# A two-layer Fourier-mixing and attention kernel: four roundings spread over four steps, statistics split, DFT weights loaded two steps later, and three output projections without maxima

## The chip, the cores and the metric

The kernel runs on one core of one Trainium2 chip. The metric is device microseconds (us) of one execution; for the kernel before there are three runs, and one more execution was profiled. TensorE is called PE here (PEld are its weight loads), VectorE DVE, ScalarE ACT, GpSimd POOL; SP is SyncE, which issues most DMAs. Each engine takes its instructions in the order in which they were written for it, so an instruction that waits holds up all that is behind it on its engine.

## The reference

All data is float32. `x` has 2048 rows (the sequence) of 512 features. Two layers, each a Fourier mixing and an attention, follow each other:

```python
def A(x):                                   # Fourier mixing, real part
    a = x @ dft_hid_re.T ; b = x @ dft_hid_im.T
    return dft_seq_re @ a - dft_seq_im @ b  # 2048 x 2048 matrices
def B(x):                                   # 32 heads of 16; one shared k and v
    q = (x @ wq) split in 32 heads ; k = x @ wk ; v = x @ wv
    p = softmax(q k^T / 4)                  # 2048 x 2048 per head
    return (p v, heads joined) @ wo
x = x + A(layernorm(x)); x = x + B(layernorm(x))
x = x + A(layernorm(x)); x = x + B(layernorm(x))
```

## The kernel before

**Products in three parts.** A float32 operand is split in a rounded part and a rest (`h` and `l`), and a product is three matmuls: h·h, h·l, l·h. Making such a pair takes a rounding (ACT, "CAST" in the trace) and a subtraction (DVE or POOL).

**The Fourier stage** (`phase_a`, once per layer) does the sequence DFT first. It has 128 steps `n`: four row blocks `tb` of the result; in each, 16 sequence blocks of the real matrix (`c` = 0), then 16 of the imaginary one (`c` = 1). In step `n` the matrix tile for step n+6 is loaded (`c_load`, into `craw`, three buffers), that for step n+2 is split (`c_split`, into `ch` on ACT and `cl` on POOL, or on DVE in the first 20 steps of layer 0; four buffers), and PE does 12 matmuls of 128 rows (tb = 0), or 24 of 64 rows (from tb = 1 on, two steps at a time, in two phases `ph`; from n = 112 on with 256 columns). They accumulate in four PSUM banks `z`, in two pairs (tile `x` in the trace). After the first phase ACT copies two columns (`junk`), and the second phase waits for that.

**The turn from c = 0 to c = 1.** After the 16th block, `evac` copies the four banks to row buffers (ACT, "ACTIVATE row<-x"), which frees the banks for c = 1, rounds all four to `zh` (ACT, "CAST slot<-row"), and subtracts for `zl` (two on POOL, two on DVE, "TENSOR_TENSOR slot<-row,slot"). All of it is written before the next steps' roundings of `ch`. The turn is taken four times in a layer.

**After c = 1** `y_rows` multiplies by the feature DFT matrix (`dh`, `dl`; loaded by `d_load`, split by `d_split` in tb = 0, in eight pieces through two row buffers, so that load j waits until piece j-2 is split), adds x (four additions on DVE, two after each PSUM pair), and takes the layernorm statistics of four tiles (`ln_stats`: bn_stats and bn_aggr), from which `ln_rstd` makes the scale. In the next row block's steps (`prep_tasks`) come transposes, k and v (`kv`, `v_tr`) and the queries (`q_mm`), which are stored to DRAM (`qd`). In layer 0, `load_wkv` at n = 20 loads the k and v weights and rounds them at once.

**Early maxima.** Softmax needs the maximum of each row of scores. A maximum is one matmul into a bank of tag `y` (three banks) or `z` (one) and one DVE reduce of 128x512. PE has room for them between the Fourier matmuls: `feed` issues a pair wherever the estimate `Pace` finds the banks free. The table `EARLY` says for which query tile and key block, in which slot, when the tile is loaded (`qT_load` at step n0), and from which place to which place (40 per row block) pairs may be fed. Which tag is taken depends on the place within the row block.

**The attention stage** (`phase_b`) has 16 query tiles of 32 steps. A step is four score matmuls, exp on ACT, four products with v (L900), and on average three of the maxima that later tiles need (`more_max`, in the order of `units`). `owed` keeps the count at 3 per step plus `o.extra`. At step 12 of tile i the projection of tile i-1 is done (`o_proj`, 12 matmuls), and after its second and fourth block two extra maxima each. A tile's maxima become mask rows (`max_neg` five steps before the tile, `max_rows`, the DMA `slot<-mt`). The query tile 13 is loaded at step 2 of tile 11, into the slot that tile 10 has just left.

Of the kernel before, what the change touches and what calls it, by code (L numbers as in the profile page):

```python
# [22 lines left out]
NT = S // P  # L23
# [9 lines left out]


EARLY = [
# [12 lines left out]
def fnet_mqa_kernel(ctx: ExitStack, tc: tile.TileContext, x_in, ct, dt_, wq, wkv, wo, out):  # L48
# [6 lines left out]
    def f(ap):  # L55
        return ap.bitcast(F32)
# [18 lines left out]
    def mm(out_, w, x, **k):  # L75
        shape_to(x.shape[0])
        Pace.pe += free(x) / 512 * (0.117 if x.shape[0] <= 64 else 0.233)
        nc.tensor.matmul(out_, w, x, **k)  # L78
# [27 lines left out]
    vec, act, pool = Timed(nc.vector, "dve"), Timed(nc.scalar, "act"), Timed(nc.gpsimd, "pool")  # L106
# [4 lines left out]
    def half(k, dtype=F32):  # L111
        return sb.tile([P, D], dtype, name=f"row{k}")
# [8 lines left out]
    def pair():  # L121
        return ps.tile([P, 2, 512], F32, name="x", bufs=2)

    def split_ps(ps_, hi, lo, neg=False):
        act.activation(hi, ps_, AF.Copy, scale=-1.0 if neg else 1.0)
        if neg:
            vec.scalar_tensor_tensor(lo, ps_, -1.0, f(hi), op0=ALU.mult, op1=ALU.subtract)
        else:
            vec.tensor_sub(lo, ps_, f(hi))

    def split_sb(raw, hi, lo, eng=None):
        act.copy(hi, raw)
        (eng or vec).tensor_sub(lo, raw, f(hi))
# [54 lines left out]
    def ln_stats(x, t):  # L188
        st = sb.tile([P, 6], F32, name="bst", bufs=2)
        vec.bn_stats(st, x)  # L190
        vec.bn_aggr(mv[:, t, :], st)
# [58 lines left out]
    def make_layer(L, src, mid, dst, last):  # L250
# [8 lines left out]
        def where(n):  # L259
            return n // 32, (n // 16) % 2, n % 16  # L260
# [27 lines left out]
        def d_load(j):  # L288
            st["d", j] = half(4 + j % 2)
            nc.sync.dma_start(st["d", j], dt_[j // NK][:, j % NK, :])  # L290

        def d_split(j):
            c, k = divmod(j, NK)
            split_sb(st["d", j], dh[c][:, k, :], dl[c][:, k, :])
# [95 lines left out]
        def partial(i):  # L390
            if i not in o.mxp:
                o.mxp[i] = sb.tile([P, NPAIR, 2, 4 if i else 5], F32, name=f"mxp{i % 4}")
                for e, (i_, kb) in enumerate(KEPT):
                    if i == i_:
                        np_ = taken[i, kb]
                        if np_:
                            pool.tensor_copy(o.mxp[i][:, :np_, :, kb], st["mxe"][:, e, :np_])
            return o.mxp[i]

        def max_pair(i, pr, c0, n, to, tags="yy"):  # L400
            pm = [bank(tag)[:, :n] for tag in tags]
            for g in range(2):
                gs = slice(64 * g, 64 * g + KR)
                mm(pm[g], o.qT[i][gs, pr, :], kz[gs, c0:c0 + n], start=True, stop=True)
            for g in range(2):
                vec.reduce_max(to[:, g:g + 1], pm[g], axis=AX.X)
                read(tags, g, Pace.dve)
# [10 lines left out]
        def feed():  # L418
            e = next((e for e in ahead if EARLY[e][4] <= Pace.at < EARLY[e][5]), None)
            if e is None:  # L420
                return
            n = Pace.at % 40
            tags = "zy" if n > 6 and Pace.z < Pace.y[1] else "yy"
            if max(Pace.z if tags == "zy" else Pace.y[1], Pace.y[0]) > Pace.pe + 0.3:
                return
            pr = ahead[e].pop(0)
            i, kb = EARLY[e][:2]
            if "mxe" not in st:
                st["mxe"] = sb.tile([P, len(KEPT), NPAIR, 2], F32, name="mxe")
            to = partial(i)[:, pr, :, kb] if i < 4 else st["mxe"][:, KEPT.index((i, kb)), pr]  # L430
            max_pair(i, pr, kb * 512, 512, to, tags)
            if not ahead[e]:
                del ahead[e]
# [48 lines left out]
        def y_rows(tb, zh, zl, x1, between):  # L482
            yp = [pair(), pair()]
            at = 0
            for ph in range(2):
                for cc in range(2):
                    for a in range(2):
                        for kk, k in enumerate((0, 2, 1, 3)):
                            for t in range(3):
                                for r in range(2):  # L490
                                    j = (r + ph) % 2
                                    rs_ = slice(64 * r, 64 * r + 64)
                                    ts_ = slice((2 * a + j) * P, (2 * a + j + 1) * P)
                                    w = (zl if t == 2 else zh)[cc][rs_, k, ts_]
                                    mm(yp[a][:, j, :], w, (dl if t == 1 else dh)[cc][rs_, k, :],
                                                     start=ph == cc == kk == t == 0, stop=cc == 1 and kk == 3 and t == 2,
                                                     skip_group_check=True)
                                between(at)
                            at += 1
                        if cc == 1 and ph == 0:  # L500
                            act.copy(junk, yp[a][:, :, 0])
                        elif cc == 1:
                            for j in range(2):
                                vec.tensor_add(x1[2 * a + j], yp[a][:, j, :], x1[2 * a + j])
                                pool.dma_start(mid[4 * tb + 2 * a + j], x1[2 * a + j])
            for tt in range(4):
                ln_stats(x1[tt], 4 * tb + tt)

        def y_tile(tb, tt, zh, zl, x1, between={}):
# [127 lines left out]
        def phase_a(extra):  # L637
# [5 lines left out]
            def add(n, fn):  # L643
                tasks.setdefault(n, []).append(fn)
# [9 lines left out]
                    add(14 + 2 * t, lambda t=t: qd_zero(t))  # L654
            add(1, d_alloc)
            for j in range(8):
                add(15 + j, lambda j=j: ((d_split(j - 2) if j > 1 else None), d_load(j)))
            add(23, lambda: d_split(6))
            add(24, lambda: d_split(7))
            inner = {}  # L660

            def by_rows(n):
# [5 lines left out]
            zh, zl, x1, vt = {}, {}, {}, {}  # L668
# [25 lines left out]
            def y_early():  # L694
                more = {k: [feed, feed] for k in (1, 4, 7)}
                y_tile(3, 0, zh, zl, x1[0], more)
                y_tile(3, 1, zh, zl, x1[1], more)
# [30 lines left out]
            held = []  # L728

            def evac(c, ds, cols):  # L730
                if cols != slice(0, 512):
                    for d in ds:
                        split_ps(z[d][:, cols], zh[c][:, d, cols], zl[c][:, d, cols], neg=c == 1)
                    return
                for k, d in enumerate(ds):
                    r = half((0 if tb == c == 0 else 4) + 2 * k + int(ds[0] > 0))
                    act.activation(r, z[d], AF.Copy, scale=-1.0 if c else 1.0)
                    held.append((d, r, vec if k and not c else pool))
                if c or len(held) == 4:
                    for d, r, eng in held:  # L740
                        act.copy(zh[c][:, d, :], r)
                        eng.tensor_sub(zl[c][:, d, :], r, f(zh[c][:, d, :]))
                    held.clear()

            def within(n, k, t):
# [34 lines left out]
            for n in range(128):  # L780
                tb, c, s = where(n)
# [12 lines left out]
                if n >= 112:  # L794
                    ch, cl = hls.pop(n)
                    h, sp = divmod(n - 112, 8)
# [59 lines left out]
        def more_max():  # L856
            if o.done < len(units) and units[o.done][0] in o.loaded | {0}:
                max_half(*units[o.done])
                o.done += 1
# [89 lines left out]
        def o_mm(k):  # L949
            if k == 0:  # L950
                bt["po"] = bank("y")
            ks = slice(k * P, (k + 1) * P)
            mm3(bt["po"], bt["oh"][:, ks], bt["ol"][:, ks], woh[:, k, :], wol[:, k, :], k == 0, k == NK - 1)

        def o_proj(i):
            for k in range(NK):
                o_mm(k)
                if k == NK - 1:
                    o_add(i)
                if k % 2 and i < NT - 1:  # L960
                    for _ in range(2):
                        more_max()
                        o.extra += 1

        def o_add(i):
            nc.vector.tensor_add(bt["x"], bt["po"], bt["x"])
            (nc.sync if last else nc.gpsimd).dma_start(dst[i], bt["x"])
# [128 lines left out]

        woh = wol = osp = None
        o.phase_a, o.phase_b = phase_a, phase_b
        return o

# [45 lines left out]
```

## Time and profile before

| what | value |
|---|---|
| runs | median 3648.55 us (3647.73 to 3650.05, 3 runs) |
| the profiled execution | 3649.77 us, its span 3648.0 us |
| granted TensorE clock, mean | 0.993 |
| busy share of the span | PE 98%, PEld 53%, DVE 77%, ACT 65%, POOL 21% |
| layer 0, Fourier stage | 0 to 664 us of the span |
| layer 0, attention stage | 664 to 1831 us |
| layer 1, Fourier stage | 1831 to 2473 us |
| layer 1, attention stage | 2473 to 3648 us |

The span runs from the first to the last instruction; what lies around it is 1.77 us in the profiled execution. A matmul counts as busy for longer than it holds up the next one: two matmuls of 64 rows run side by side, and a pair of them follows the pair before after 0.233 us, though each is shown with 0.39 us. So time that PE loses is read from the idle times in brackets, from the starts of matmuls, and from the granted clock.

### The profile page before, as it was taken

The numbers are of one execution on the slowest core, as the hardware profiler recorded it, in microseconds if no ns is written. First come the engines' busy times: TensorE is split into PE (matmuls) and PEld (weight loads), VectorE is DVE, ScalarE is ACT, GpSimd is POOL, SyncE is SP. The second block draws the span as 40 slices with busy tenths as digits, with TensorE's granted clock in tenths as the row PEclk, the third lists the DMA queues.
The fourth block names the chain that finished last, engine by engine and source line by source line (L and its number), as shares of the span: only waits on it lengthen the run. The fifth ranks groups of instructions, "written<-read, shape, count | busy, mean of one in ns | idle before, by whom it ended". The sixth has DMA issues, their size and how long they took to land.

```text
span 3648.0 us, 63760 instructions
## 1 busy us (share of the span) xinstructions
PE 3571.4 (98%) x25090; PEld 1924.1 (53%) x25090; DVE 2801.7 (77%) x4819; ACT 2389.4 (65%) x3058; POOL 782.6 (21%) x976
## 2 busy tenths in 40 slices
PE   8999999999999999999999999999999999999999
PEld 6777878434333333334377878773343334333433
DVE  6176988888888888888311869878888888888881
ACT  3322232788888888888943232328888888888888
POOL 5544342111121112111254343420000000000000
PEclk9999999999999999999999999999999999999999
DMA  5544242311111100110143343422111111001100
GB/s 171 133 149 122 88 128 73 85 48 34 36 34 39 43 25 22 31 51 22 42 128 104 122 127 103 130 65 75 47 36 34 34 48 34 25 21 50 33 24 26
DMA packets 204445, 240.85 MB, mean 66 GB/s; under 512 B 36848, under 2 KB 160752, under 8 KB 197232
## 3 DMA queue, kind: packets, MB, share of 16 engines
q1 hardware_dynamic: 199216, 219.98, 20.3%
q0 software_dynamic: 4864, 16.78, 1.6%
q8 instruction: 196, 3.21, 0.4%
q14 instruction: 105, 0.86, 0.1%
q10 hardware_dynamic: 64, 0.02, 0.0%
HBM read 172.48 MB, written 63.17 MB: 65 GB/s over the span
## 4 chain that ended last, share of the span: by engine, by line
PE 84%; DVE 7%; ACT 2%; issue 1%; DMA 1%; SPq 0%; POOL 0%; ACTq 0%; DVEq 0%; POOLq 0%
PE z L900 26%; PE y L78 19%; PE x L886 19%; PE x L78 17%; DVE mxp L102 4%; PE z L78 1%; DVE mxe L102 1%; ACT slot L889 1%; ACT slot L881 0%; DVE slot L102 0%; PE z L83 0%; DMA slot<-qd 0%; PE y L879 0%; DVE bst L102 0%; DVE row L102 0%
## 5 line engine op out<-in xcount | busy, mean ns | idle before, releaser
L102 DVE TENSOR_REDUCE mxp<-y 128x1 f32<-128x512 f32 (+1 forms) x3464 | 2160.9, 678 | 271.8 <-PE y L78 216.5
L889 ACT ACTIVATE slot<-x 128x1024 f32<-128x1024 f32 x1984 | 1938.2, 1028 | 327.3 <-PE x L886 249.8
L900 PE MATMUL z<-slot,v 128*32 128x512 f32 x8192 | 1097.8, 606 | 2.4 <-ACT row L903 2.4
L78 PE MATMUL y<-kz,slot 64*128 64x512 f32 (+1 forms) x3040 | 984.3, 426 | 10.1 <-DMA slot<-qd 4.3
L886 PE MATMUL x<-slot,kz 64*128 64x512 f32 x2944 | 886.8, 448 | 2.8 <-DMA slot<-mt 2.7
L886 PEld LDWEIGHTS x<-slot,kz 64*128 64x128 f32 x2944 | 367.1, 185 | 734.3 <-ACT slot L889 594.6
L78 PE MATMUL x<-ch,xnh 64*128 64x512 f32 (+2 forms) x2048 | 543.5, 374 | 22.6 <-ACT xnh L102 9.4
L78 PEld LDWEIGHTS y<-kz,slot 64*128 64x128 f32 x3040 | 490.1, 186 | 126.6 <-DVE mxp L102 32.2
L78 PE MATMUL x<-ch,xnl 64*128 64x512 f32 (+2 forms) x2048 | 540.6, 367 | 1.7 <-POOL xnl L102 1.2
L78 PE MATMUL x<-cl,xnh 64*128 64x512 f32 (+2 forms) x2048 | 536.7, 366 | 1.7 <-POOL cl L102 1.6
L940 POOL TENSOR_TENSOR row<-row,row 128x256 f32<-128x256 f32 x63 | 46.2, 733 | 1581.6 <-DMA row<-rd 987.4
L102 POOL TENSOR_TENSOR cl<-craw,ch 128x512 fp32r<-128x512 f32 x244 | 317.6, 1318 | 288.2 <-ACT ch L102 259.4
L78 PEld LDWEIGHTS x<-ch,xnh 64*128 64x128 f32 (+1 forms) x2048 | 304.7, 187 | 76.0 <-issue 16.2
L78 PEld LDWEIGHTS x<-ch,xnl 64*128 64x128 f32 (+1 forms) x2048 | 310.7, 187 | 37.1 <-POOL xnl L102 5.0
L78 PEld LDWEIGHTS x<-cl,xnh 64*128 64x128 f32 (+1 forms) x2048 | 306.7, 187 | 33.6 <-POOL cl L102 2.9
L900 PEld LDWEIGHTS z<-slot,v 128*32 128x32 f32 x8192 | 164.4, 108 | 276.1 <-issue 248.1
L102 ACT CAST ch<-craw 128x512 fp32r<-128x512 f32 x264 | 158.6, 620 | 173.1 <-PE x L78 152.9
L102 ACT COPY junk<-x 128x2 f32<-128x2 f32 x236 | 37.6, 159 | 354.7 <-PE x L78 336.3
L102 DVE TENSOR_REDUCE mxe<-y 128x1 f32<-128x512 f32 x408 | 256.1, 676 | 6.4 <-PE y L78 6.1
L78 PE MATMUL y<-slot,slot 128*128 128x512 f32 x816 | 218.2, 407 | 9.4 <-DVE mxp L102 7.1
L78 PEld LDWEIGHTS y<-slot,slot 128*128 128x128 f32 x816 | 144.3, 188 | 65.6 <-issue 29.5
L102 DVE TENSOR_REDUCE mxp<-z 128x1 f32<-128x512 f32 x128 | 86.8, 678 | 91.6 <-PE y L78 87.6
(126 smaller groups left out, 2676.9 us busy)
## 6 DMA issues: line engine op xcount, KB each, us to landing
craw<-ct_in SPq DMA_DIRECT2D x112, 512.0 KB
slot<-qd SPq DMA_DIRECT2D x42, 1024.0 KB
qd<-row SPq DMA_DIRECT2D x144, 128.0 KB
od<-row SPq DMA_DIRECT2D x252, 64.0 KB
row<-x_in SPq DMA_DIRECT2D x32, 256.0 KB
mid<-row POOLq DMA_DIRECT2D x32, 256.0 KB, 2.5
craw<-ct_in SPq DMA_DIRECT2D x32, 256.0 KB
row<-mid SPq DMA_DIRECT2D x32, 256.0 KB
```

Of the source, the lines that this page charges most:

```text
L78: nc.tensor.matmul(out_, w, x, **k)
L102: return fn(out_, in_, *a, **k)
L886: nc.tensor.matmul(st["e"][:, g, :], kz[64 * g:64 * g + KR, c * P:(c + 1) * P], o.qT[i][64 * g:64 * g + KR, cp:cp + 4, :], start=True, sto ...
L889: nc.scalar.activation(ptiles[i, s_][:, 2 * w:2 * w + 2, :], st.pop("e"), AF.Exp, scale=DH ** -0.5)
L900: nc.tensor.matmul(a[32 * j:32 * j + 32, :], v1[:, c, :], pt[:, j, :], start=c == 0, stop=c == NT - 1)
L940: nc.gpsimd.tensor_mul(bt["ot"][:, cs], bt["ot"][:, cs], bt["den"][:, cs])
```

## The change

Five things change:

- The table's first four entries (tiles 2, 3, 0 and 1, key block 0) may be fed from 55.5, 60, 63 and 66 on instead of 54.5, 58, 60 and 63, and the bank `z` is used for maxima only from place 7 of a row block on, not from 6.
- In `y_rows` the statistics of the first tile are taken between the first two additions and the last two.
- `d_load` and `d_split` come two steps later (loads at n = 17 to 24).
- At the turn from c = 0, the four roundings with their subtractions are handed out to the steps n+1 to n+4, one to each.
- The projections of tiles 0, 1 and 2 have no extra maxima, and `o.extra` isn't counted up there.

```diff
-    (2, 0, 2, 43, 54.5, 70), (3, 0, 3, 46, 58, 70), (0, 0, 8, 48, 60, 89), (1, 0, 9, 52, 63, 91),
+    (2, 0, 2, 43, 55.5, 70), (3, 0, 3, 46, 60, 70), (0, 0, 8, 48, 63, 89), (1, 0, 9, 52, 66, 91),
...
-            tags = "zy" if n > 6 and Pace.z < Pace.y[1] else "yy"
+            tags = "zy" if n > 7 and Pace.z < Pace.y[1] else "yy"
...
                                 pool.dma_start(mid[4 * tb + 2 * a + j], x1[2 * a + j])
-            for tt in range(4):
+                            if a == 0:
+                                ln_stats(x1[0], 4 * tb)
+            for tt in range(1, 4):
                 ln_stats(x1[tt], 4 * tb + tt)
...
-                add(15 + j, lambda j=j: ((d_split(j - 2) if j > 1 else None), d_load(j)))
-            add(23, lambda: d_split(6))
-            add(24, lambda: d_split(7))
+                add(17 + j, lambda j=j: ((d_split(j - 2) if j > 1 else None), d_load(j)))
+            add(25, lambda: d_split(6))
+            add(26, lambda: d_split(7))
...
             def evac(c, ds, cols):
+                zh_, zl_ = zh.get(c), zl.get(c)
...
+                def low(d, r, eng):
+                    act.copy(zh_[:, d, :], r)
+                    eng.tensor_sub(zl_[:, d, :], r, f(zh_[:, d, :]))
+
+                if c:
+                    for h in held:
+                        low(*h)
+                elif len(held) == 4:
+                    for k, h in enumerate(held):
+                        add(n + 1 + k, lambda h=h: low(*h))
                 if c or len(held) == 4:
-                    for d, r, eng in held:
-                        act.copy(zh[c][:, d, :], r)
-                        eng.tensor_sub(zl[c][:, d, :], r, f(zh[c][:, d, :]))
                     held.clear()
...
-                if k % 2 and i < NT - 1:
+                if k % 2 and 3 <= i < NT - 1:
                     for _ in range(2):
                         more_max()
                         o.extra += 1
```

The numbers of instructions stay nearly the same: one pair of early maxima fewer in each layer, and two maxima more in its attention stage.

Where the instructions stand shows at three places. The first is ACT at the first turn (tb = 0, layer 0), from the four evacuations on. `slot_622` is `zh`, `slot_278` and `slot_280` are the DFT weights, `ch` is the next steps' matrix. Before:

```order
L102 ACTIVATE row_642<-x 128x512
L102 CAST slot_622<-row_630 128x512
L102 CAST slot_622<-row_632 128x512
L102 CAST slot_622<-row_640 128x512
L102 CAST slot_622<-row_642 128x512
L102 CAST ch<-craw 128x512 x2
L102 CAST slot_278<-row_652 128x512
L102 CAST ch<-craw 128x512
L102 CAST slot_278<-row_676 128x512
L102 CAST ch<-craw 128x512
L102 CAST slot_278<-row_696 128x512
L102 CAST wkvh<-row_760 128x512
```

After:

```order
L102 ACTIVATE row_642<-x 128x512
L102 CAST ch<-craw 128x512
L102 CAST slot_622<-row_630 128x512
L102 CAST ch<-craw 128x512
L102 CAST slot_622<-row_632 128x512
L102 CAST ch<-craw 128x512
L102 CAST slot_622<-row_640 128x512
L102 CAST ch<-craw 128x512
L102 CAST slot_278<-row_684 128x512
L102 CAST slot_622<-row_642 128x512
L102 CAST ch<-craw 128x512
L102 CAST wkvh<-row_752 128x512
```

A rounding of the matrix stands between any two of the turn's roundings, and ahead of the k and v weights (`wkvh`) stands one piece of the DFT weights instead of three.

The second is ACT at the turn of tb = 1, layer 0; `slot_1860` is `zh`. Before:

```order
L102 ACTIVATE row_1952<-x 128x512
L102 CAST slot_1860<-row_1928 128x512
L102 CAST slot_1860<-row_1930 128x512
L102 CAST slot_1860<-row_1950 128x512
L102 CAST slot_1860<-row_1952 128x512
L102 CAST ch<-craw 128x512 x2
L102 COPY junk<-x 128x2 x2
```

After:

```order
L102 ACTIVATE row_1940<-x 128x512
L102 CAST ch<-craw 128x512 x2
L102 COPY junk<-x 128x2 x2
L102 CAST slot_1860<-row_1902 128x512
L102 CAST slot_1860<-row_1904 128x512
L102 CAST ch<-craw 128x512 x2
L102 COPY junk<-x 128x2 x2
```

The roundings of `ch` and the copy that lets the second phase begin have moved ahead of the four.

The third is PE in step 5 of tile 11 of layer 0's attention stage. The second operand of an L78 row is the query tile whose maxima are taken. Before (`slot_14407` is tile 12, `slot_16856` is tile 13):

```order
L900 MATMUL z<-slot_16862,v_74 32x512 x4
L886 MATMUL x<-slot_13589,kz 128x512
L78 MATMUL y<-kz,slot_14407 128x512
L886 MATMUL x<-slot_13589,kz 128x512
L78 MATMUL y<-kz,slot_16856 128x512 x2
L886 MATMUL x<-slot_13589,kz 128x512 x2
```

After (`slot_14365` is tile 12; L896 and L910 are the L886 and L900 of before):

```order
L910 MATMUL z<-slot_16820,v_74 32x512 x4
L896 MATMUL x<-slot_13547,kz 128x512
L78 MATMUL y<-kz,slot_14365 128x512
L896 MATMUL x<-slot_13547,kz 128x512
L78 MATMUL y<-kz,slot_14365 128x512 x2
L896 MATMUL x<-slot_13547,kz 128x512 x2
```

Tile 12's maxima are still going on; tile 13's first one stands five steps later, in step 10.

## The prediction

> **What bounds the kernel now.** I read the page first: busy shares and the chain of work that ended last.
>
> ```profile
> PE 3571.4 (98%) x25090; PEld 1924.1 (53%) x25090; DVE 2801.7 (77%) x4819; ACT 2389.4 (65%) x3058; POOL 782.6 (21%) x976
> ...
> PE 84%; DVE 7%; ACT 2%; issue 1%; DMA 1%; SPq 0%; POOL 0%; ACTq 0%; DVEq 0%; POOLq 0%
> ```
>
> PE is the bound nearly everywhere, and the change takes only a fraction of a microsecond of matmuls away. So it can gain only time in which PE stands still or runs slowly, and that is short: what matters is which waits these are. The table of PE's waits (first 130 to 664 us, layer 0's Fourier stage; then 1831 to 2473, layer 1's) gives total, count and longest:
>
> ```profile
> PE x L78 <- ACT junk L102: 4.2, 4, 1.4
> PE z L78 <- DMA slot<-qd: 3.4, 1, 3.4
> PE z L83 <- DVE row L102: 2.5, 3, 0.8
> ...
> PE z L83 <- DVE mxp L102: 0.7, 1, 0.7
> ```
>
> ```profile
> PE x L78 <- ACT junk L102: 4.3, 4, 1.4
> PE z L83 <- DVE row L102: 2.6, 3, 0.9
> ```
>
> (The row on `z L83 <- DVE mxp` reads the same in layer 1.) Each of these names a place that the change touches. Two costs stand beside them: an earlier wait at 80 us, and the granted clock, which falls to half for some microseconds behind longer waits. I take the parts in the order of the program.
>
> **(a) DFT weights later, first turn of layer 0.** Timeline of SP, ACT and PE, then busy times with the clock:
>
> ```profile
> 69.94 0.33 SPq L290 DMA_DIRECT2D row<-dt_in  x1
> ...
> 76.66 0.42 SPq L185 DMA_DIRECT2D row<-wkv_in  x1
> 74.43 0.62 ACT L102 CAST slot<-row 128x512 fp32r<-128x512 f32 x1 [8.09 <-DMA row<-dt_in]
> 82.05 0.62 ACT L102 CAST wkvh<-row 128x512 fp32r<-128x512 f32 x1 [6.47 <-DMA row<-wkv_in]
> 83.76 0.80 PE L78 MATMUL x<-ch,xnh 128*128 128x512 f32 x1 [3.81 <-ACT ch L102]
> 84.00:90.00 6.00, 5.36 (x13) 3.84 (x14) 2.12 (x2) 1.90 (x5) 5.08 (x5) 0.53 0.54 167
> ```
>
> ACT waits 8.09 us for the third piece of the DFT matrix, whose load could be issued only at 69.94, when the first piece had been split. SP is held by these loads, and so issues the load of the k and v weights at 76.66 only; ACT, which rounds them at once, stands until 82.05, and the next `ch` is behind it. PE loses 3.81, and then 6 us at a clock of 0.53 lose 6 x 0.47 = 2.8: 6.6 in all. Changed, SP has two loads fewer ahead of the k and v weights, and ACT one piece of DFT weights instead of three. The last thing SP waits for is then the split of the first piece, in step 19. A step is 12 x 0.233 = 2.8 us, and ACT works about one step ahead of PE: PE's step 23 was due at 79.8, so ACT's step 19 falls near 67 and the load is issued near 69. With the latency seen (82.05 - 76.66 = 5.4) it lands near 75, and the `ch` that PE needs at 79.8 is rounded by about 77. Gain 6.6. Ends: 0, if the load still comes late, and 7. The later pieces now wait up to step 26; PE needs them in `y_rows` after step 31, and ACT's cover is the one step by which `ch` runs ahead. Without it each late piece would cost PE what it is late.
>
> **(b) Tile 2's first maxima one step later.** The chain, PE's timeline and the clock:
>
> ```profile
> 193.78 6.07 DMA slot<-qd
> 199.98 0.76 PE L78 MATMUL z<-kz,slot 64*128 64x512 f32 x1 [3.42 <-DMA slot<-qd]
> 200.00:206.00 6.00, 6.00 (x30) 5.11 (x32) 3.88 (x7) 0.16 (x1) 0.00 (x0) 0.52 1.02 427
> ```
>
> The load lands at 199.85 and PE has waited 3.42. The load's place is not moved; the first maximum stands one step, 24 matmuls x 0.117 = 2.8 us, later. 0.6 us of the wait stay, and I take it that the clock doesn't fall for so little: 2.8 + 6 x 0.48 = 5.7. Ends 2.8 (the clock falls all the same) and 6.3. In layer 1 this wait isn't in the table, so nothing there. The other three entries move alike; their tail runs 24 matmuls further into `y_rows`, where DVE is idle.
>
> **(c) The turns.** ACT, DVE and PE at the turn of tb = 1, one subtraction alone elsewhere, the turn at n = 112; then PE's and DVE's busy times, (x) counts instructions, the number behind POOL's is the clock:
>
> ```profile
> 208.96 2.18 ACT L102 CAST slot<-row 128x512 fp32r<-128x512 f32 x4
> 210.20 3.00 DVE L102 TENSOR_TENSOR slot<-row,slot 128x512 fp32r<-128x512 f32 x2 [1.83 <-ACT slot L102]
> 75.09 0.69 DVE L102 TENSOR_TENSOR slot<-row,slot 128x512 fp32r<-128x512 f32 x1 [4.57 <-ACT slot L102]
> 212.29 0.50 PE L78 MATMUL x<-ch,xnh 64*128 64x512 f32 x2 [1.08 <-ACT junk L102]
> 542.97 0.39 PE L78 MATMUL x<-ch,xnh 64*128 64x256 f32 x2 [1.43 <-ACT junk L102]
> ```
>
> ```profile
> 209.00:219.00 10.00, 7.98 (x63) 5.40 (x61) 8.80 (x12) 4.63 (x11) 7.29 (x6) 1.00 0.17 56
> 219.00:229.00 10.00, 10.00 (x89) 8.42 (x88) 10.00 (x18) 1.88 (x6) 3.76 (x3) 1.00 0.50 175
> 372.00:382.00 10.00, 8.08 (x52) 5.79 (x50) 9.09 (x12) 3.82 (x9) 6.63 (x5) 0.83 0.15 52
> 2019.00:2029.00 10.00, 7.99 (x50) 5.57 (x49) 8.79 (x12) 3.62 (x9) 6.65 (x5) 0.83 0.24 85
> ```
>
> Undisturbed, 10 us hold 89 matmuls. The turn at 209 has 63 and loses 26/8.9 = 2.9; the turns at 372 and 2019 lose 37/8.9 = 4.2 and 4.4, of which 10 x 0.17 = 1.7 is a fallen clock. The fourth (layer 1, tb = 2) I take like the first: 14.4 together. Two causes: the `junk` copy is behind four roundings (it comes forward, so that wait goes), and DVE, idle 1.83 for the first rounding, then takes 3.00 for two subtractions while maxima are due. DVE is busy 10.00 of 10 afterwards, so what it loses itself PE does not get back. Spread, DVE's idle time goes; the two subtractions cost between 2 x 0.69 and 3.00, so of the 2.9 between 1.3 and 2.9 come back. I take 2.1, the middle: POOL, whose subtractions coincide with DVE's where it is slow, is busy 7.29 of 10 in the turn's window and 3.76, half of that, in the next, into which the change moves them. 4 x 2.1 + 2 x 1.4 for the clock = 11.2. At n = 112 only the `junk` wait counts: 1.43, twice with layer 1: 2.9. Sum 14.1; ends 8.1 (four times 1.3, no clock) and 17.3. The row buffers are held up to four steps longer; their next users (row block inputs, transposes) come 10 steps later.
>
> [...]
>
> **(d) Statistics split.** DVE's timeline at the end of tb = 0:
>
> ```profile
> 131.92 1.29 DVE L102 TENSOR_TENSOR row<-x,row 128x512 f32<-128x512 f32 x2 [37.48 <-PE x L78]
> 134.54 1.29 DVE L102 TENSOR_TENSOR row<-x,row 128x512 f32<-128x512 f32 x2 [1.33 <-issue]
> 135.74 0.68 DVE L102 BATCH_NORM_STATS2 bst<-row 128x6 f32<-128x512 f32 x1
> 136.56 0.66 DVE L102 BATCH_NORM_STATS2 bst<-row 128x6 f32<-128x512 f32 x1
> ```
>
> One tile's statistics take 136.56 - 135.74 = 0.82 and fit in the 1.33 that DVE waits. All behind them, to the transposes, comes 0.82 earlier; each of the six waits `z L83 <- DVE row` is about 0.83, so 6 x 0.8 = 4.8 go. Ends 3 and 4.9.
>
> **(e) Bank `z` from place 7 on.** The transposes of v need the bank that a maximum has just taken: 0.7 in each layer, 1.4. End 0, if DVE is late with the `y` banks instead.
>
> **(f) to (h) The attention stage.** PE's timeline in tile 11 of both layers, then chain rows: a projection with and one without extra maxima, two steps in a row with three maxima and two without:
>
> ```profile
> 1483.80 0.80 PE L78 MATMUL y<-kz,slot 64*128 64x512 f32 x2 [3.13 <-DMA slot<-qd]
> 3290.95 0.50 PE L78 MATMUL y<-kz,slot 64*128 64x512 f32 x2 [1.15 <-DMA slot<-qd]
> ```
>
> ```profile
> 1276.17 4.06 PE y L78 x16
> 1792.23 3.00 PE y L78 x12
> 1271.72 0.99 PE z L900 x8
> 1273.84 1.00 PE z L900 x8
> 1780.77 1.04 PE z L900 x8
> 1782.66 1.04 PE z L900 x8
> ```
>
> (f) Tile 13's first maximum waits 3.13 and 1.15 for its load. Twelve extra maxima fewer and two units more put it five steps of 1273.84 - 1271.72 = 2.12 later, 10 us: both waits go, and with the first a clock fall, priced at 2.8 like (a): 7.1. (g) Three projections shorter by 4.06 - 3.00 = 1.06, in two layers: 6.4. (h) The 14 maxima come at the end, where a step of 1.89 becomes one of 2.12: 14 x 0.23 / 3 = 1.1, twice: -2.2. Ends for the three: 8 and 12.
>
> **Sum.** 6.6 + 5.7 + 14.1 + 4.8 + 1.4 + 7.1 + 6.4 - 2.2 = 43.9. The profiled execution took 3649.77, 1.77 of it around its span and 1.2 above the median: 3605.9 on its scale, 3604.7 on the median's. I say 3604.5.
>
> **Rivals.** (1) The first turn's wait only moves: load 69 plus a latency as for the third piece, or a later piece holds `ch`. Then (a) is 0: 3611. The 8.09 and 6.47 of ACT speak for it, the two steps won against it. (2) DVE keeps the turns: its 10.00 of 10 speaks for it. (c) falls to 8.1: 3610.5. (3) The change doesn't do what it says in the Fourier stage: the moved maxima meet DVE or their loads a step later, so that (b), (c) and (e), 21.2, are given back: 3626. Against it: the waits have other causes than the amount of maxima. (4) Slower: the maxima lose their lead. The last one of tile 14 stands 4.5 steps ahead of its `max_neg` now, and directly ahead of it then; if mask rows came late at every boundary, PE would wait there, which now costs 2.7 us in all:
>
> ```profile
> L886 PE MATMUL x<-slot,kz 64*128 64x512 f32 x2944 | 886.8, 448 | 2.8 <-DMA slot<-mt 2.7
> ```
>
> One step late, 2.1, at 30 boundaries is 64 us: 3668. It decides from 1.5 us a boundary on (44/30). Against it: DVE takes its work in order and had other tiles' maxima before `max_neg` anyway.
>
> **Chances.** Forecast 0.64, own range 3597 to 3613 (ends of (b) and (c)); rival 1 0.12, rival 2 0.13, rival 3 0.06, slower 0.02, about nothing 0.03. 0.2% (7 us) is about what a measurement can tell from no change. Faster 0.95, same 0.03, slower 0.02. The range: all upper ends give 3600, and the waits not priced here a little less; the lower ends of (a) and (c) together give 3617; 3597 to 3620 leaves out rivals 3 and 4.
>
> **What would show it.** Right: no wait of PE for ACT near 80 us and none over 1 us near 197; no `ACT junk` wait at the turns of n = 48, 80, 112; `z L83 <- DVE row` near 0.1 each; no `slot<-qd` wait in tile 11; projections of tiles 0 to 2 as x12. Wrong: new waits of PE for `DVE mxp` in the turns, `slot<-dt` waits on ACT that reach PE, or `slot<-mt` waits at many boundaries.

## The result, and the profile after

| | before | changed |
|---|---|---|
| median (runs) | 3648.91 us (3647.73 to 3650.05, 4) | 3601.3 us (3600.53 to 3602.6, 4) |
| ratio, 95% interval | | 0.987 (0.9853 to 0.9887) |
| profiled execution / span | 3649.77 / 3648.0 | 3602.02 / 3600.2 |
| mean granted clock | 0.993 | 0.997 |
| layer 0 Fourier, attention | 664.4, 1166.9 | 641.2 (-23.2), 1159.0 (-7.8) |
| layer 1 Fourier, attention | 641.6, 1162.8 | 630.0 (-11.7), 1157.8 (-5.0) |

A stage is counted here from the last exp of the attention stage before it (or the span's start) to its first exp, an attention stage from its first to its last exp. The changed kernel is faster by 47.6 us; the forecast was 3604.5, range 3597 to 3620. The terms of the prediction, laid out by stage, are 22.4, 8.0, 10.1 and 3.3: each stage gained about what it was to gain, the two of layer 1 some 1.7 more.

The page after, then PE's waits in 130 to 629 us (layer 0), then in 1795 to 2436 us (layer 1):

```profile
PE 3551.6 (99%) x25090; PEld 1901.3 (53%) x25090; DVE 2801.6 (78%) x4819; ACT 2390.8 (66%) x3050; POOL 781.9 (22%) x976
...
PE 85%; DVE 7%; ACT 2%; issue 1%; DMA 1%; SPq 0%; POOL 0%; DVEq 0%; ACTq 0%; POOLq 0%
```

```profile
PE z L83 <- DVE row L102: 2.0, 3, 0.8
...
PE x L78 <- ACT junk L102: 0.7, 1, 0.7
...
PE z L78 <- DMA slot<-qd: 0.2, 1, 0.2
```

```profile
PE z L83 <- DVE row L102: 2.1, 3, 0.9
...
PE x L78 <- ACT junk L102: 0.7, 1, 0.7
```

Of the `junk` waits one is left in each layer (step 120, not a turn; 0.66). The wait for `slot<-qd` fell from 3.4 to 0.2, that for `mxp` at `z L83` (0.7) is gone. What did not go is the row on `z L83 <- DVE row`: 2.5 became 2.0, where 0.3 was expected.

Windows of the changed kernel: around the first turn's old wait, behind tile 2's first maxima, and around the four later turns (now 8 to 31 us earlier); the clock is the number behind POOL's count:

```profile
74.00:84.00 10.00, 10.00 (x45) 8.10 (x44) 3.44 (x4) 4.16 (x8) 5.33 (x5) 1.00 0.54 170
200.00:206.00 6.00, 6.00 (x56) 5.13 (x54) 5.97 (x11) 2.60 (x6) 3.99 (x3) 1.00 0.34 111
...
201.00:211.00 10.00, 10.00 (x88) 8.27 (x88) 9.97 (x17) 3.38 (x8) 6.76 (x5) 1.00 0.43 161
360.00:370.00 10.00, 9.53 (x80) 7.76 (x78) 9.97 (x16) 3.29 (x8) 5.76 (x5) 1.00 0.20 63
1994.00:2004.00 10.00, 9.89 (x84) 7.48 (x83) 10.00 (x17) 2.76 (x7) 4.20 (x4) 1.00 0.57 209
2152.00:2162.00 10.00, 9.53 (x80) 7.57 (x78) 10.00 (x15) 2.81 (x8) 5.40 (x4) 1.00 0.17 52
```

The turns hold 88, 80, 84 and 80 matmuls where before held 50 to 63, and no clock falls in them. The two with 80 are those of tb = 2: there PE still waits 0.37 for a maximum (`mxe`) in each layer, where before it waited 0.84. In the chain of work, the projection of tile 0: in a kernel with the old projections (told of below), then in the changed one:

```profile
739.05 4.06 PE y L78 x16
```

```profile
739.10 2.97 PE y L78 x12
```

In tile 11 the table of PE's waits has no row on `slot<-qd` left.

### The profile page after: what moved, and what is told of

Its sections match the earlier page's. It is cut to its first block, busy times and chain, and to the rows that moved or that the text cites. A ratio compares the mean times of both kernels' runs of the same rounds, so it can differ in the third digit from the quotient of the medians.

```text
span 3600.2 us, 63751 instructions
## 1 busy us (share of the span) xinstructions
PE 3551.6 (99%) x25090; PEld 1901.3 (53%) x25090; DVE 2801.6 (78%) x4819; ACT 2390.8 (66%) x3050; POOL 781.9 (22%) x976
## 4 chain that ended last, share of the span: by engine, by line
PE 85%; DVE 7%; ACT 2%; issue 1%; DMA 1%; SPq 0%; POOL 0%; DVEq 0%; ACTq 0%; POOLq 0%
PE z L910 27%; PE y L78 19%; PE x L896 19%; PE x L78 17%; DVE mxp L102 4%; PE z L78 1%; DVE mxe L102 1%; ACT slot L899 1%; PE z L83 1%; ACT slot L891 0%; PE y L889 0%; DVE row L102 0%; DVE bst L102 0%; DVE ms L102 0%; PE y L83 0%
## 5 line engine op out<-in xcount | busy, mean ns | idle before, releaser
L910 PE MATMUL z<-slot,v 128*32 128x512 f32 x8192 | 1096.4, 605 | 1.7 <-ACT row L913 1.7
L78 PE MATMUL y<-kz,slot 64*128 64x512 f32 (+1 forms) x3048 | 980.1, 424 | 4.4 <-DVE kz L102 2.1
L896 PE MATMUL x<-slot,kz 64*128 64x512 f32 x2960 | 891.2, 447 | 0.8 <-DMA slot<-mt 0.8
L896 PEld LDWEIGHTS x<-slot,kz 64*128 64x128 f32 x2960 | 368.1, 185 | 734.3 <-ACT slot L899 599.7
L78 PEld LDWEIGHTS y<-kz,slot 64*128 64x128 f32 x3048 | 487.8, 185 | 121.8 <-DVE mxp L102 26.5
L78 PE MATMUL x<-ch,xnh 64*128 64x512 f32 (+2 forms) x2048 | 531.6, 372 | 11.7 <-ACT xnh L102 9.5
L78 PE MATMUL x<-ch,xnl 64*128 64x512 f32 (+2 forms) x2048 | 527.8, 364 | 1.0 <-POOL xnl L102 0.6
L78 PE MATMUL x<-cl,xnh 64*128 64x512 f32 (+2 forms) x2048 | 524.3, 364 | 0.4 <-POOL cl L102 0.4
L78 PEld LDWEIGHTS x<-ch,xnh 64*128 64x128 f32 (+1 forms) x2048 | 293.1, 185 | 63.4 <-issue 16.2
L78 PEld LDWEIGHTS x<-ch,xnl 64*128 64x128 f32 (+1 forms) x2048 | 298.7, 185 | 38.0 <-POOL xnl L102 4.4
L78 PEld LDWEIGHTS x<-cl,xnh 64*128 64x128 f32 (+1 forms) x2048 | 295.0, 185 | 32.2 <-POOL cl L102 0.7
L910 PEld LDWEIGHTS z<-slot,v 128*32 128x32 f32 x8192 | 163.7, 108 | 274.6 <-issue 247.5
L78 PE MATMUL y<-slot,slot 128*128 128x512 f32 x816 | 216.4, 406 | 8.2 <-DVE mxp L102 6.7
L78 PEld LDWEIGHTS y<-slot,slot 128*128 128x128 f32 x816 | 144.7, 188 | 63.1 <-issue 28.2
L896 PE MATMUL x<-xnl,kz 64*128 64x512 f32 x512 | 154.5, 443 | 0.3 <-DMA xnl<-mt 0.3
```

Source lines behind the costliest of these rows:

```text
L896: nc.tensor.matmul(st["e"][:, g, :], kz[64 * g:64 * g + KR, c * P:(c + 1) * P], o.qT[i][64 * g:64 * g + KR, cp:cp + 4, :], start=True, sto ...
L910: nc.tensor.matmul(a[32 * j:32 * j + 32, :], v1[:, c, :], pt[:, j, :], start=c == 0, stop=c == NT - 1)
```

## The experiments

Each kernel's time is a median, of runs taken beside runs of the kernel before. The changed kernel itself was run again with the second and the third group, to be held against on the same chip.

### The parts alone, in the kernel before

**The turn alone.**

```diff
 (kernel before, with the new evac)
...
+                    for k, h in enumerate(held):
+                        add(n + 1 + k, lambda h=h: low(*h))
```

> The kernel before with one part of the change alone: the four roundings of a turn handed out to the steps n+1 to n+4. Theory (term c): every ACT junk wait at the turns of n = 48, 80 and 112 goes, and with it the DVE mxp or mxe wait behind it (0.84) and the fallen clock; between 14.1 and 17.3 us come back: 3632 to 3635. The wait of PE for ACT near 80 us of layer 0 (3.8, and a halved clock behind it) stays, since the DFT weights are loaded as before. Rival (DVE keeps the turns): 8.1 come back, 3641, and mxp or mxe waits of 0.8 stay at the turns.

Measured 3624.48 us (ratio 0.9934, 0.9922 to 0.9947): 24.9 less, far more than 17.3. Its waits, layer 0:

```profile
PE z L78 <- DMA slot<-qd: 4.7, 1, 4.7
PE z L83 <- DVE row L102: 2.5, 3, 0.8
...
PE x L78 <- POOL cl L102: 0.9, 1, 0.9
...
PE z L83 <- DVE mxp L102: 0.7, 1, 0.7
```

```profile
78.89 0.62 ACT L102 CAST wkvh<-row 128x512 fp32r<-128x512 f32 x1 [7.63 <-DMA row<-wkv_in]
```

The `junk` waits at the turns and the maxima's waits of 0.84 behind them are gone. In layer 1, where nothing else differs, the stage is 6.9 shorter. Taken from the wait of one row block's transposes (`z L83`, behind `y_rows`) to that of the next, its three later row blocks gained 3.3 (1.7 of it a clock fall that is gone), 1.7 and 2.4, or 7.4 in all, where term (c) has 7.05 for a layer. The first row block gained 1.0 (a wait of 0.6 for `cl` is gone), and behind the last of these waits 1.5 is lost, where the clock of this run falls once more, at 2429 us.

The 2.4 are the turn at n = 112, for which the prediction counted only the wait of 1.43. The stretch from the wait ahead of it to the one at step 120, before and then here:

```profile
540.33 0.39 PE L78 MATMUL x<-ch,xnh 64*128 64x256 f32 x2 [0.24 <-ACT row L102]
586.51 0.39 PE L78 MATMUL x<-ch,xnh 64*128 64x256 f32 x2 [0.66 <-ACT junk L102]
```

```profile
528.23 0.39 PE L78 MATMUL x<-ch,xnh 64*128 64x256 f32 x2 [0.23 <-ACT row L102]
571.93 0.39 PE L78 MATMUL x<-ch,xnh 64*128 64x256 f32 x2 [0.66 <-ACT junk L102]
```

It holds the same 498 matmuls, 54 of them for maxima, and takes 46.18 us before and 43.70 here; in layer 1 46.10 and 43.70. So 1.0 more than the wait is lost before: behind it the two matmuls of a pair of maxima start up to 0.6 apart (545.04 and 545.64), here together (529.87 and 529.88).

Layer 0 is 15.9 shorter: 5.3 up to the first `z L83` (though this run began 1.0 later, by PE's wait at 20 us), 2.9, 3.9 and 2.5 in the three later row blocks, and 1.4 behind them, where a clock fall at 642 us is gone. In the 2.9 lies tile 2's wait, here 4.7 instead of 3.4, with half as much time at half speed behind it as the 6.83 us of before. The 5.3 are most of term (a): the expectation that the wait near 80 us stays was wrong. ACT rounds the first DFT piece no earlier than before (64.05, against 64.16), but DVE no longer has the turn's two subtractions ahead of this piece's own one. That ends at 65.65 instead of 69.91, and SP issues the next load right behind it. So the k and v weights come at 78.9 instead of 82.05, and only a wait of 0.9 is left, for `cl`.

**All four roundings together, but one step later.**

```diff
-                    for k, h in enumerate(held):
-                        add(n + 1 + k, lambda h=h: low(*h))
+                    for k, h in enumerate(held):
+                        add(n + 1, lambda h=h: low(*h))
```

(The lines taken out are those of the turn alone.)

> The kernel before with the four roundings put behind the next step's work, but all four in step n+1 instead of one to a step. Theory: only the copy ahead of the second phase needs to come forward, so the junk waits (1.08 at four turns, 1.43 at two) go, and the two clock falls (1.4 each): 4.3 + 2.9 + 2.8 = 10 come back, and the DVE wait of 0.84 behind each turn stays, since DVE still takes its two subtractions together: about 3639. Rival: the DVE waits are a consequence of the junk wait or of the late roundings ahead of it and go too: then it is as fast as with four steps, 3632 to 3635, and the spreading itself is worth nothing.

Measured 3640.82 us (0.9982, 0.9973 to 0.999): 8.5 less. Its waits, and DVE at the turn of tb = 1:

```profile
PE x L78 <- ACT ch L102: 3.5, 1, 3.5
PE y L78 <- DVE mxe L102: 2.8, 6, 1.1
...
PE z L78 <- DVE mxp L102: 1.4, 1, 1.4
```

```profile
212.64 3.02 DVE L102 TENSOR_TENSOR slot<-row,slot 128x512 fp32r<-128x512 f32 x2 [0.71 <-ACT slot L102]
```

No `junk` wait is left at a turn, but DVE's two subtractions together still take 3.02 us and PE's wait for a maximum is 1.35 and 1.12 instead of 0.84. The first turn's wait stays (3.5), and a clock fall with it. So bringing the copy forward is worth a third to a half (8.5 of the 18.3 that the four steps give without the first turn's 6.6), and spreading the rest. Spread, the two subtractions take 0.69 and 1.19 us in the changed kernel:

```profile
202.02 0.69 DVE L102 TENSOR_TENSOR slot<-row,slot 128x512 fp32r<-128x512 f32 x1
209.81 1.19 DVE L102 TENSOR_TENSOR slot<-row,slot 128x512 fp32r<-128x512 f32 x1
```

**The DFT weights alone.**

```diff
-                add(15 + j, lambda j=j: ((d_split(j - 2) if j > 1 else None), d_load(j)))
+                add(17 + j, lambda j=j: ((d_split(j - 2) if j > 1 else None), d_load(j)))
...
```

> The kernel before with the loads and splits of the DFT weights two steps later, and nothing else. Theory (term a): it is SP, held by two loads more, that makes the load of the k and v weights late; two steps later the 3.81 wait near 80 us and the halved clock behind it go, 6.6 us: 3642. Rival: the four roundings of the turn, which stand together on ACT there, or the late first piece keep ACT late, so that the wait stays in part, and only both edits together take it away: 3645 to 3649.

Measured 3646.27 us (0.9991, 0.9982 to 1.0), 3.1 less, not surely different from before. The 3.81 is gone, but in the profiled execution, the fastest of eleven, a wait of 2.6 stands earlier, from 65.8 us on:

```profile
PE x L78 <- ACT junk L102: 4.3, 4, 1.4
PE x L78 <- DVE cl L102: 2.6, 1, 2.6
```

DVE there, then DVE in the kernel before:

```profile
62.15 3.08 DVE L102 TENSOR_TENSOR slot<-row,slot 128x512 fp32r<-128x512 f32 x2 [5.38 <-ACT slot L102]
65.15 4.90 DVE L102 TENSOR_TENSOR cl<-craw,ch 128x512 fp32r<-128x512 f32 x2
```

```profile
65.24 2.39 DVE L102 TENSOR_TENSOR cl<-craw,ch 128x512 fp32r<-128x512 f32 x2
```

DVE still splits the matrix there, and in both kernels it has the turn's two subtractions just ahead. But the first `cl` takes 3.20 us (65.15 to 68.35) where it took 0.68 before, and PE waits for it. POOL's own subtraction runs beside it from 65.64 to 66.92; that may explain a part, which no run shows by itself, and the rest stays open. Neither theory had this. The clock differs too: this run has falls at four turns, before at two. So the load's shift by itself removes the wait near 80 us, but of its 6.6 only 3.1 show in the median, and the turn alone brings most of it.

### Statistics and the stores

**Statistics together again in the changed kernel.**

```diff
-                            if a == 0:
-                                ln_stats(x1[0], 4 * tb)
-            for tt in range(1, 4):
+            for tt in range(4):
```

> The changed kernel with the statistics taken together behind the four additions again. Term (d) of the prediction gave the split 4.8 us: by it this kernel takes 3606.1. Theory now: the six waits of the transposes for DVE's rows are near 0.83 each (two of them were 0.37 with the split), so only 0.9 us are lost: 3602.2, and DVE's lnv operation takes about 0.2 us again, since POOL's two subtractions have ended when it begins.

Measured 3604.67 us, beside 3649.36 of before: 44.7 less, where the changed kernel had 47.6 less than its own before. That is 2.9 worse, but across two groups of runs, and the changed kernel itself took 3600.5 to 3604.3 in three. So the waits have to settle it: `z L83 <- DVE row` is 2.5 and 2.6 again, 0.9 more in all, and `lnv` takes 0.16 to 0.21 in these places. What else differs is a wait of 1.2 for tile 2's load and another clock fall at the end of layer 1's stage, neither of them work of the statistics; both vary between runs of one kernel.

**The stores issued by SP instead of POOL**, with the split statistics and without:

```diff
-                                pool.dma_start(mid[4 * tb + 2 * a + j], x1[2 * a + j])
+                                nc.sync.dma_start(mid[4 * tb + 2 * a + j], x1[2 * a + j])
```

> The changed kernel once more, for the next three to be held against on the same chip. 3601.3 is expected, within 1.5.

> The changed kernel with the stores of the new rows (mid) issued by SP instead of POOL, in all six y_rows. Theory of why term (d) failed: POOL takes its work in order, so its two cl subtractions stand behind these stores until the last addition, run 2.57 us long beside DVE's small lnv operation and hold it until they end. With the stores gone from POOL the subtractions run earlier, lnv takes 0.2 instead of 1.01 us, four of the z L83 waits for DVE's rows (0.83, 0.83, 0.92, 0.83) fall to about 0.1 and the other two (0.37) stay: 3 us less than the changed kernel on this chip. Rival: lnv waits for something else (the last statistics' write, say), and its end stays where it is: no difference, and the waits stay at 0.83.

> As the one before, but with the statistics taken together again. Theory: DVE's own order of work is then what ends last, 0.82 later, whatever POOL does: all six waits near 0.83, lnv 0.2 us, and with the row before it the split is worth about 4 us once POOL is out of the way. Rival: POOL's place matters by itself (the waits fall without the split), and this one is as fast as the one before.

On this chip the changed kernel takes 3603.78 us (3602.13 to 3604.27), 2.5 more than in its first runs, where 1.5 was allowed for; with SP's stores 3600.28 (3598.8 to 3602.04), with these and statistics together 3602.62 (3599.88 to 3605.19). POOL and DVE behind `y_rows` of tb = 0 in the changed kernel's first run, then DVE with SP's stores:

```profile
129.01 2.57 POOL L102 TENSOR_TENSOR cl<-craw,ch 128x512 fp32r<-128x512 f32 x2
```

```profile
130.60 1.01 DVE L102 TENSOR_SCALAR lnv<-mv 128x4 f32<-128x4 f32 x1
```

```profile
131.40 0.17 DVE L102 TENSOR_SCALAR lnv<-mv 128x4 f32<-128x4 f32 x1
```

`lnv` works on 4 values a row. Beside POOL's subtraction it ends at 131.61, POOL's second at 131.58; without, it takes 0.17. PE's six waits for DVE's rows, in order: split and POOL 0.83, 0.83, 0.38, 0.92, 0.83, 0.38; split and SP none, none, 0.37, 0.73, none, 0.38; together and SP all six 0.78 to 0.87. So the gain needs both: DVE's own order and POOL's place were two limits that ended at the same time, and the change moved one. The 0.37 stay since two early maxima stand ahead of `lnv` there; the 0.73 is ACT loading its square root's table, here with SP's stores (the last experiment takes both away):

```profile
1919.60 1.28 ACT L102 ACT_TABLE_LOAD   x1
1920.89 0.21 ACT L102 ACTIVATE lnw<-lnv 128x4 f32<-128x4 f32 x1
```

**POOL's subtractions done twice.**

```diff
+                if n % 32 in (2, 3) and 32 < n < 128:
+                    pool.tensor_sub(hls[n][1], raws[n // 2][:, n % 2, :], f(hls[n][0]))
```

> The changed kernel with POOL's two cl subtractions behind y_rows (steps 34, 35, 66, 67, 98 and 99) done twice, the second time with the same result. Theory: DVE's lnv operation is held until POOL's subtractions end, so it takes about 2.6 us longer (3.6 instead of 1.01) for tb = 0 and 1, and the waits of the transposes grow from 0.83 to about 3.4; for tb = 2, where lnv begins after POOL's end now, by about 2.3: some 15 us more and clock falls of 1.7 on top, 3616 to 3626. Rival: lnv's 1.01 has nothing to do with POOL, and the doubled work is hidden as far as PE is concerned: the same time, lnv 1.01.

Measured 3611.84 us (one run), span 3610.1: 9.8 more than the changed kernel, not 15.

```profile
130.60 1.12 DVE L102 TENSOR_SCALAR lnv<-mv 128x4 f32<-128x4 f32 x1
132.00 0.18 DVE L102 RECIPROCAL rs<-lnw 128x4 f32<-128x4 f32 x1 [0.27 <-ACT lnw L102]
132.22 0.78 DVE L102 TENSOR_TENSOR lnw<-rs 128x4 f32<-128x4 f32 x1
133.03 0.16 DVE L102 TENSOR_TENSOR lnw<-lnw,lnv 128x4 f32<-128x4 f32 x1
133.22 1.12 DVE L102 TENSOR_SCALAR lnw<-lnw 128x4 f32<-128x4 f32 x1
```

```profile
129.02 5.30 POOL L102 TENSOR_TENSOR cl<-craw,ch 128x512 fp32r<-128x512 f32 x4
```

The four subtractions begin at 129.02, 130.40, 131.65 and 133.06, and POOL's next work at 134.26. DVE's operation is held until the one that runs then has ended (131.72, 133.00, 134.34), gets in between two, and the next is held again. So it is a hold for one operation, not for the whole of POOL's work: the waits grew to 2.50 for tb = 0 and 1 (2.62 once) and 1.9 for tb = 2, not to 3.4, and that was the miss. Together the six are 13.9 us instead of 4.2, which is the whole of the 9.8. The rival (nothing to do with POOL) is out.

### Early maxima and projections

**The first four entries as before.**

```diff
-    (2, 0, 2, 43, 55.5, 70), (3, 0, 3, 46, 60, 70), (0, 0, 8, 48, 63, 89), (1, 0, 9, 52, 66, 91),
+    (2, 0, 2, 43, 54.5, 70), (3, 0, 3, 46, 58, 70), (0, 0, 8, 48, 60, 89), (1, 0, 9, 52, 63, 91),
```

> The changed kernel with the first four entries of the table of early maxima as before (54.5, 58, 60, 63). Term (b): tile 2's first maximum waits about 3 us for its load again near 190 us and the clock falls behind it: 3.4 to 5.7 more than the changed kernel. Rival: the load now lands in time, or other work moves into the place, and nothing is lost. In layer 1 nothing moves by either.

Measured 3609.45 us (3604.21 to 3610.95) against 3603.78 on this chip: 5.7 more, and the two profiled executions are 6.4 apart. Layer 0's Fourier stage has 3.3 of that:

```profile
PE z L78 <- DMA slot<-qd: 4.5, 1, 4.5
```

With the clock at half for 3.4 us behind it that is the wait of term (b); the changed kernel waited 1.9 here in this group's run, 0.2 in the first. Another 2.7 are in layer 1's Fourier stage, where nothing was expected: 1.0 in tb = 1, where a maximum waits 0.35 for DVE, and 1.4 at the stage's end, where the clock falls once more. I can't tell these apart from what a further run would give.

**The projections with their extra maxima.**

```diff
-                if k % 2 and 3 <= i < NT - 1:
+                if k % 2 and i < NT - 1:
```

> The changed kernel once more, for the next three to be held against on the same chip: 3601 to 3604.

> The changed kernel with the extra maxima in the projections of tiles 0, 1 and 2 as before. Terms (f) to (h): tile 13's first maximum waits for its load again in tile 11 (about 3.1 and 1.1, and a clock fall if the whole wait lies in one stretch of 3.4 us), three projections are 1.06 longer in each layer, and the 14 maxima at the end are not there: 7.1 + 6.4 - 2.2 = 11.3 more than the changed kernel by the prediction; by the lengths of the tiles in the two traces, 12.8. The Fourier stages don't change. Rival: the wait for the load was a matter of the DMA queue, not of where the maximum stands, and doesn't return: 4 more.

Measured 3609.34 us (3605.08 to 3610.23) against 3602.17 of the changed kernel on this chip: 7.2 more, between the theory's 11.3 and the rival's 4. Counted by the products with v, tiles 1 to 3 (with the projections of tiles 0 to 2 in them) are 1.13, 1.25 and 1.24 longer in layer 0, 1.32, 1.33 and 1.52 in layer 1; the last tile is 1.1 and 1.4 shorter. In tile 11 the wait for the load does not return:

```profile
1459.67 0.50 PE L78 MATMUL y<-kz,slot 64*128 64x512 f32 x2 [0.19 <-DMA slot<-qd]
```

Its load was issued at 1454.72, 4.8 us ahead of where PE wanted it, against 2.4 in the kernel before. So the projections are not needed for it. The first maximum stands one step later than before, by the two maxima more that the changed table leaves to the attention stage, and one step was nearly enough; that it is these two is read from the order, and no run has them alone.

**More of the same.**

```diff
 (the changed kernel with SP's stores, and)
-    (2, 0, 2, 43, 55.5, 70)
+    (2, 0, 2, 43, 56.5, 70)
...
+            if L:
+                add(20, lambda: act.activation(junk[:, :1], kone, AF.Sqrt))
...
+                if n == 96 and k < 4:
+                    return
```

> The changed kernel with four edits: the stores of the new rows issued by SP (3.3 less, as before), the table's first entry from 56.5 on (tile 2's first maximum waited 0.2 and 1.9 for its load in two runs of the changed kernel: 1 less on average), no early maximum in the first phase of step 96, so that none stands ahead of lnv at tb = 2 (2 x 0.37), and in layer 1 one square root of a single column at step 20, so that ACT loads its table (1.28 us) before the first lnw needs it (0.73). Together 5.8 less than the changed kernel on this chip. Against it: the two moved maxima take time elsewhere, and 4 to 5 remain.

Measured 3600.14 us (3598.29 to 3600.63) against 3602.17 (3601.13 to 3603.15): 2.0 less, where 5.8 was expected. All six waits for DVE's rows are gone, but at tb = 2 another stands in their place in both layers:

```profile
PE y L78 <- DVE mxe L102: 0.6, 1, 0.6
```

So the three further edits take away the waits that they were made for, but in the time nothing of them can be shown beyond SP's stores. Both kernels with these stores and the split statistics beat the changed kernel beside which they ran.

## Why the prediction was right

- **(a), 6.6.** Right in size: no wait is left, the load of the k and v weights goes out at 70.33 and lands by 75.78, where 69 and 75 were forecast (SP, then ACT):

```profile
70.33 0.42 SPq L185 DMA_DIRECT2D row<-wkv_in  x1
```

```profile
75.78 0.62 ACT L102 CAST wkvh<-row 128x512 fp32r<-128x512 f32 x1 [6.59 <-DMA row<-wkv_in]
```

  The attribution was half right: the turn alone removes all but 0.9 of the wait, through DVE, which the prediction didn't look at here, and with the shift alone 2.6 stood elsewhere. Counted once, the sum was right.
- **(b), 5.7.** The wait and the clock fall are gone; undoing it gave back 3.3 in layer 0. The 0.6 that was to remain is 0.2, 0.5 and 1.9 in the changed kernel's three profiled executions: it hangs on when the DMA lands. With the old entries it was 3.4 to 4.7 in four profiles, but 0.5 in the fifth (the DFT weights alone), so part of this term is a matter of chance.
- **(c), 14.1.** Right in mechanism, and near in size: the turn's own experiment gives 7.4 in layer 1's three later row blocks, and 3.9 and 2.5 in the two of layer 0 that nothing else disturbs. The turn at n = 112 was priced too low, 1.43 where it gave 2.4 and 2.5; of the others, the two with a clock fall gave 3.3 and 3.9, where 3.5 was priced, and one without 1.7, where 2.1 was. Rival 2 (DVE keeps the turns) is out; its half of the story is the kernel with all four in one step. Of this sum the clock's 2.8 is not the change's alone (last section).
- **(d), 4.8: the step that failed.** 0.9 to 1.0. "All behind them comes 0.82 earlier" left out POOL: its subtraction ran beside the four values of `lnv` and held them. Before, `lnv` began as the subtraction ended, so no wait showed:

```profile
139.06 0.21 DVE L102 TENSOR_SCALAR lnv<-mv 128x4 f32<-128x4 f32 x1
```

```profile
136.67 2.55 POOL L102 TENSOR_TENSOR cl<-craw,ch 128x512 fp32r<-128x512 f32 x2
```

  The end of POOL's pair, 139.22, and lnv's, 139.27, stood in the rows and were not held against each other.
- **(e), 1.4.** The 0.7 is gone in every kernel with the new rule for the tags, also with the old entries, statistics or projections, and is there in every one without, also with the turn or the shift alone; no run has the rule alone.
- **(f) to (h), 11.3.** 12.8 by the stages. Mis-sized: (g) is 1.1 to 1.5 a projection, not 1.06 (its own row gives 1.09, 4.06 against 2.97; where the rest comes from isn't shown); (f)'s gain didn't need the projections, as the prediction had it; (h) is 1.1 and 1.4 a layer, near the 1.1 said.
- **What the sum left out.** (d) gave 3.9 too little, and yet the span is 3.9 shorter than the sum had it, so 7.8 came from elsewhere. The attention stages have 1.5 of that. About 6 lie in the Fourier stages. 2.0 of them are the turn at n = 112 in both layers, shown in the turn's own experiment. The others were not tried by themselves: waits of 0.6 for `cl` at the first turn of both layers that are gone, tile 2's wait, of which 0.2 stayed instead of 0.6, the two clock falls at the turns, 1.7 each instead of 1.4, and a pair of maxima fewer in each layer (0.24 where its matmuls start together, 1.2 where they stand alone, 0.6 apart). What is left, under 2 us, I can't place. (d) and these parts pull the sum in opposite directions; that they partly cancel is luck.

## What to carry to other kernels

When an instruction is to come earlier, look at what else ends at the same time as it does now, on every engine that can hold it: two limits that end together (before, POOL's pair at 139.22 and `lnv` at 139.27) show one wait, and moving one of them showed little (0.9 to 1.0 us where 4.8 was forecast). A wait behind a batch of work went when the batch was spread over steps; moved as a whole by one step, the batch still held the engine that does its second half (DVE's 3.02 us, with waits of 1.35 and 1.12 behind it). The cost of a wait can be larger than its idle time, when the order behind it is disturbed (at n = 112 the wait was 1.43 and the gain 2.4), so measure it from the wait ahead to the next one. And a gain that is measured for a whole change should be taken apart in both directions, since two edits can each remove the same wait (the 3.81 near 80 us).

## What the runs showed of the hardware

**The clock falls on a grid.** In all 14 profiles the starts of the half-speed stretches lie on one grid of 3.413 us in each run (within 6 ns), and each is one to four pieces of it long (the last one, cut off by the end, aside). In the kernel before, the first three begin at 82.83, 198.89 and 376.38 us, 34 and 52 pieces apart. Two turns of the kernel before, cut on that grid:

```profile
209.10:212.50 3.40, 2.32 (x22) 1.62 (x20) 2.30 (x2) 3.29 (x8) 2.85 (x2) 1.00 0.01 2
212.50:215.90 3.40, 2.46 (x17) 1.38 (x17) 3.40 (x6) 0.00 (x0) 3.08 (x3) 1.00 0.01 2
373.00:376.40 3.40, 1.48 (x10) 0.57 (x6) 3.40 (x4) 1.72 (x5) 3.40 (x3) 1.00 0.00 0
376.40:379.80 3.40, 3.40 (x15) 2.45 (x16) 3.17 (x6) 0.00 (x0) 1.51 (x2) 0.50 0.25 86
```

The same two waits, 1.08 and 0.84: at 209 they lie in two pieces and nothing falls, at 373 in one, and the next piece runs at half speed. Of the pieces at full clock with 1.92 us of idle PE or more (the span's first 15 us and its last pieces aside) all 13 were followed by a fall (in the kernel before 2.88 at 79.42, 2.32 at 195.47 and 1.92 at 372.96 us); away from the ends of the Fourier stages none with under 1.2 was; between, both happened (in the kernel before 1.54 at 540.22 without a fall, 1.62 at 1478.88 with one). So a wait of 2 us costs 2 or 3.7 (one piece at half speed loses 3.413 / 2 = 1.7) by chance, which the prediction took for a property of a turn. The kernel before, with many such waits, ranged from 3644.6 to 3653.5 in all its runs, the changed kernel from 3600.5 to 3604.3. The mean granted clock of the 35 runs of the kernel before goes with it: at 0.994 they took 3645.6 us on average (4 runs), at 0.992 3650.8 (10 runs). No piece had to be idle as a whole for a fall: 1.92 us of idle PE in the 3.413 from 372.96 on were enough.

**Which small operations are held.** Behind `y_rows` in the changed kernel, in the one with the first four entries as before and in the one with POOL's subtractions done twice, DVE's TENSOR_SCALAR beside POOL's subtraction took 0.99 to 1.14 and TENSOR_TENSOR 0.70 to 0.78, for 4 values a row (0.16 or 0.17 where they began just ahead of POOL's next one); RECIPROCAL took 0.18 and BATCH_NORM_STATS2 0.66 or 0.67 there, no longer than without it (0.18, and 0.66 to 0.70).
